# Score matmuls of 64 rows instead of zero-padded ones, values summed key tile by key tile, and a re-planned order, in a kernel of normalized attention and a gated feed-forward layer

## The chip, the cores and the metric

The kernel runs on one core of one Trainium2 chip. The metric is the device time of one execution in microseconds (us). The kernel before was timed three times: 449.11, 449.39 and 452.02 us, median 449.39 us. One more execution was profiled; the profile's times below are of that one.

## The reference: what is computed

There are 8 batches, 12 heads, 448 positions and 64 numbers per head. Attention comes first, then a feed-forward layer over all 3584 tokens:

```
q_n, k_n = rmsnorm(q, g_q), rmsnorm(k, g_k)          # over the 64 numbers of a head
attn = softmax(q_n @ k_n.T / sqrt(64))                # 448 x 448 for each of 96 heads
x = (attn @ v), heads side by side                    # 3584 x 768
h = x @ w_in                                          # 768 -> 2048
out = (h * clip(h + 3, 0, 6) / 6) @ w_out             # 2048 -> 768
```

All inputs and the output are float32 in memory. The matmuls take bfloat16 operands.

## The kernel before

**Pairs.** Two heads are handled together, which fills 2 x 64 = 128 rows; there are 48 pairs, 6 to a batch. The 448 positions of a head are 3 full tiles of 128 rows and a rest of 64. The two rests of a pair share one tile (number 3), so a pair has 7 key tiles: 0 to 2 of the first head, 3 with both rests, 4 to 6 of the second head.

**Stages of a pair.** k, q and v are loaded for two pairs at a time (a group) into rings of three staging buffers `k_st`, `q_st`, `v_st`. `square` (L309) and `stats_sum` (L317) make sums of squares, `stats_rstd` (L323) the factors 1/rms on ACT. `normalize` (L332) multiplies k and q by them. In pairs 0 to 13 (`TD = 14`) `transposes` (L346) turns them on PE into the PSUM tile `t_ps`; `put_q` (L381) and `put_k` (L387) copy them out into `kq`. From pair 14 on a DMA transpose does this instead (`transposes_dma`, L377), into a copy of the same layout that POOL has written, and `scale_q` on ACT multiplies q by the gains.

**The padded k.** The part of `kq` called `kpad` holds 7 blocks of 128 columns. Rows 0 to 63 belong to the first head and rows 64 to 127 to the second. A block of tiles 0 to 2 has the first head's k in the upper rows and zeros below; a block of tiles 4 to 6 the reverse; block 3 holds both rests. q of both heads stands below each other in the same 128 rows. So each score matmul (`score`, L392) contracts over 128 rows, half of them zeros in six cases of seven. `clear_k` (L507) writes the zeros once for each of three ring buffers; `put_k` makes two copies of 64 rows per pair.

**Scores, weights, values.** Each score matmul writes one of two PSUM banks (`sc`), and `expo` (L398) on ACT makes the exponentials `eT` from it, one of a ring of 14. With two banks, score number m waits for exponential m-2. When all seven exponentials of a pair are there, `weigh` (L405) multiplies them with the values and a column of ones: for each of four query tiles seven matmuls, one of 130 columns and six of 65, in two halves of two query tiles. They sum into one PSUM tile `av`. `divide` (L425) on DVE divides by the sums of exponentials, which frees `av`. The result is transposed (`x_out`, by PE until pair 13, by DMA after) into `xT`.

**Feed-forward.** For a finished batch, 16 items of six matmuls (`h_mm`, L460) with `relu` on ACT and `gate` on DVE, and then items of 16 matmuls (`y_mm`, L477), each copied out by ACT or DVE and stored. The weights are loaded in 16 pieces of 768 KB through three buffers `w_st` and cast to bfloat16 by POOL, DVE or ACT; the same three buffers are the source of the DMA transposes from pair 14 on, so pair 14 can be normalized only after the last weight is cast.

**What sets the order.** Nothing runs in the order of the loops. Each piece of work is entered in a list with a key (a due time), the engines that could do it with an assumed time on each, and the pieces it depends on. `Plan.run` (L115) then plays time forward: when an engine is free it takes the ready piece with the smallest key, and each piece goes to the engine where its assumed end (weighted by `PRICE`) is earliest. Ready attention work on PE goes ahead of feed-forward matmuls as long as a credit is not negative; `share` sets how fast feed-forward work refills it. What comes out is a fixed order of instructions on each engine. On the chip each engine runs its list in this order and waits where something is not ready yet; the DMA issues on SP are such a list, too.

## Time and profile before

| view | what it says |
|---|---|
| times | 449.11, 449.39, 452.02 us |
| profiled execution | span 449.5 us from the first to the last instruction |
| PE | busy 424.5 us (94%), 3512 matmuls, first one 9.86 us after the start |
| DVE, ACT, POOL | busy 240.1, 274.8 and 229.7 us (53%, 61%, 51%) |
| score matmuls (L393) | 336, each of 448 columns, 8.2 us of waiting before them |
| feed-forward matmuls (L461, L480) | 768 of 448 columns and 896 of 384 columns |
| value matmuls (L413, L419) | 192 of 130 columns and 1152 of 65 columns |
| exponentials (L399) | 336 on ACT, 175.7 us, 48.6 us of waiting before them |
| copies of k out of `t_ps` (L390) | 28 on DVE, 11.7 us |
| casts of v (L280) | 29 on POOL of 618 ns, 10 on DVE of 1145 ns, 9 on ACT of 627 ns |
| DMA | 73.94 MB, queue q1 69.3% of 16 engines' span |

An instruction's row gives its own duration, from start to end. Matmuls overlap: the next one starts before the last one has ended, so the distance from start to start (the pitch), which the timeline shows, is what a matmul costs when PE is full. "Idle before, releaser" says how long the engine stood still before the instructions of a group, and what ended most of that. The granted clock (PEclk) is the share of full speed at which PE ran.

### The profile page before, as it was taken

The page shows a single profiled execution, that of the slowest core. Times are in us where ns is not written, and L with a number is a line of the kernel's source. Part 1 is how long each engine was busy: PE and PEld are TensorE (multiplying, and loading weights), DVE is VectorE, ACT ScalarE, POOL GpSimd, SP SyncE. Part 2 cuts the span into 40 slices and gives each one's busy share as a digit, 9 for nine tenths or more (in the row PEclk, how much of TensorE's full clock was granted, in tenths as well). Part 3 has the DMA queues.
Part 4 walks back from the last instruction along what each step waited for, and adds up shares of the span by engine and source line. Part 5 has one row for each costly group of instructions (what it writes and reads, how often), then busy time and mean ns, then how long its engine had stood idle before and what let it go on. Part 6 is the DMA issues. An engine that isn't in the chain of part 4 may idle for free.

```text
span 449.5 us, 9164 instructions
## 1 busy us (share of the span) xinstructions
PE 424.5 (94%) x3512; PEld 255.4 (57%) x3512; DVE 240.1 (53%) x428; ACT 274.8 (61%) x581; POOL 229.7 (51%) x251
## 2 busy tenths in 40 slices
PE   0888799899999989999999999999999999999996
PEld 0455366565566555666566565656565655555563
DVE  6899888845474346646444555453433253343321
ACT  2678678853487678878776777777767551132100
POOL 5899999958577766855667467552310000000000
PEclk9999899999999999999999999999999999999999
DMA  6899999981999999999899777955545210110021
GB/s 160 208 295 247 306 294 283 309 296 47 216 229 191 227 231 199 169 232 188 160 184 219 177 176 171 223 140 76 93 106 72 73 26 36 61 45 36 24 83 70
DMA packets 140908, 73.94 MB, mean 164 GB/s; under 512 B 90176, under 2 KB 137280, under 8 KB 140864
## 3 DMA queue, kind: packets, MB, share of 16 engines
q1 hardware_dynamic: 139232, 72.44, 69.3%
q10 hardware_dynamic: 1632, 0.92, 0.8%
q8 instruction: 27, 0.44, 0.4%
q14 instruction: 17, 0.14, 0.1%
HBM read 45.61 MB, written 11.01 MB: 126 GB/s over the span
## 4 chain that ended last, share of the span: by engine, by line
PE 84%; DMA 6%; POOL 2%; DVE 2%; ACT 2%; SPq 1%; issue 1%; POOLq 0%
PE m L461 29%; PE m L480 26%; PE sc L393 11%; PE av L419 7%; PE sc L480 5%; DMA k_st<-in_k_dram 4%; DMA kq<-w_st 3%; PE sc L461 3%; PE av L413 2%; ACT eT L399 2%; POOL qk L333 1%; POOL sq L315 1%; DVE vaug L280 1%; PE t_ps L349 1%; SPq L277 0%
## 5 line engine op out<-in xcount | busy, mean ns | idle before, releaser
L399 ACT ACTIVATE eT<-sc 128x448 bf16<-128x448 f32 x336 | 175.7, 542 | 48.6 <-PE sc L393 44.6
L461 PE MATMUL m<-xT,w_in_sb 128*128 128x448 bf16 x708 | 165.7, 355 | 0.2
L480 PE MATMUL m<-w_out_sb,gT 128*128 128x384 bf16 x768 | 150.0, 326 | 0.0
L393 PE MATMUL sc<-kq 128*128 128x448 bf16 x336 | 115.9, 359 | 8.2 <-ACT eT L399 6.4
L480 PEld LDWEIGHTS <-gT 128*128 128x128 bf16 x896 | 87.2, 98 | 62.3 <-issue 0.5
L461 PEld LDWEIGHTS <-w_in_sb 128*128 128x128 bf16 x768 | 74.1, 98 | 68.8 <-issue 6.0
L472 DVE SCALAR_TENSOR_TENSOR gT<-t_sb,m 128x448 bf16<-128x448 f32 x118 | 73.0, 620 | 72.9 <-ACT t_sb L467 72.4
L467 ACT ACTIVATE t_sb<-m 128x448 f32<-128x448 f32 x118 | 63.7, 541 | 47.3 <-PE m L461 44.3
L318 DVE TENSOR_REDUCE ssq<-sq 128x16 f32<-128x1024 f32 (+1 forms) x56 | 58.3, 1058 | 8.4 <-POOL sq L315 7.1
L359 POOL TENSOR_TENSOR w_st<-k_st,rstd 128x256 bf16<-128x256 f32 x68 | 40.2, 612 | 41.3 <-DMA kq<-w_st 40.6
L280 DVE COPY y_sb<-m 128x384 f32<-128x384 f32 x39 | 21.7, 557 | 61.4 <-PE m L480 61.2
L419 PE MATMUL av<-vaug,eT 128*128 128x65 bf16 x1152 | 54.5, 194 | 0.0
L419 PEld LDWEIGHTS <-eT 128*128 128x128 bf16 x1152 | 50.8, 99 | 4.4 <-issue 0.4
L315 POOL TENSOR_TENSOR sq<-k_st 128x1024 f32<-128x1024 f32 (+1 forms) x24 | 42.4, 1765 | 12.7 <-DMA k_st<-in_k_dram 5.9
L315 POOL TENSOR_TENSOR sq<-q_st 128x1024 f32<-128x1024 f32 (+1 forms) x26 | 44.5, 1710 | 7.1 <-DMA q_st<-in_q_dram 3.5
L393 PEld LDWEIGHTS <-kq 128*128 128x128 bf16 x336 | 31.3, 99 | 27.0 <-issue 4.9
L413 PE MATMUL av<-vaug,eT 128*128 128x130 bf16 x192 | 42.7, 222 | 0.0
L280 POOL CAST vaug<-v_st 128x512 bf16<-128x512 f32 x29 | 17.9, 618 | 45.2 <-PE av L419 44.6
L367 POOL TENSOR_TENSOR w_st<-q_st,rstd 128x512 bf16<-128x512 f32 x34 | 35.4, 1042 | 0.0
L429 DVE TENSOR_TENSOR xn<-av,rden 128x512 bf16<-128x512 f32 x48 | 33.2, 691 | 1.7
L428 DVE RECIPROCAL rden<-av 128x8 f32<-128x8 f32 x48 | 9.8, 205 | 34.1 <-PE av L419 33.7
L375 ACT ACTIVATE kq<-kq,gprime 128x448 bf16<-128x448 bf16 x34 | 22.6, 663 | 5.1 <-DMA kq<-w_st 5.1
(55 smaller groups left out, 222.5 us busy)
## 6 DMA issues: line engine op xcount, KB each, us to landing
out_dram<-y_sb SPq DMA_DIRECT2D x24, 384.0 KB, 2.9
k_st<-in_k_dram SPq DMA_DIRECT2D x23, 384.0 KB, 4.6
v_st<-in_v_dram SPq DMA_DIRECT2D x23, 384.0 KB, 4.6
q_st<-in_q_dram SPq DMA_DIRECT2D x22, 384.0 KB, 4.7
w_st<-in_moe_w_in_dram SPq DMA_DIRECT2D x8, 768.0 KB, 7.6
w_st<-in_moe_w_out_dram SPq DMA_DIRECT2D x8, 768.0 KB, 7.1
out_dram<-y_sb SPq DMA_DIRECT2D x8, 192.0 KB, 2.7
k_st<-in_k_dram SPq DMA_DIRECT2D x46, 32.0 KB, 3.9
```

Source lines behind the costliest of these rows:

```text
L280: (eng.copy if eng is nc.scalar else eng.tensor_copy)(out=out, in_=in_)
L315: eng.tensor_tensor(out=sq, in0=x, in1=x, op=A_MULT)
L318: nc.vector.tensor_reduce(out=ssq_r[(p // GP) % 2][:, a, p % GP:p % GP + n, :].rearrange("p r s -> p (r s)"), in_=sq_r[m][:, 0:n].rearrang ...
L359: eng.tensor_tensor(out=blocks[:, c0:c0 + W4].rearrange("p (t c) -> p t c", t=4)[:, :, h * D:(h + 1) * D], in0=raw(0, p, 1)[:, 0, 4 * h:4 ...
L393: nc.tensor.matmul(out=sc_r[n % 2][:, 0:S], lhsT=kpad[p % NK][:, i * P:(i + 1) * P], rhs=qT_r[p % NK], start=True, stop=True,)
L399: nc.scalar.activation(out=eT_r[n % NE][:, 0:S], in_=sc_r[n % 2][:, 0:S], func=EXP, bias=0.0, scale=1.0,)
L413: nc.tensor.matmul(out=av_ps[:, i, 0:2 * W], lhsT=e[3][:, cols], rhs=va[:, 3].rearrange("p h d -> p (h d)"), start=True, stop=False, skip_ ...
L419: nc.tensor.matmul(out=av_ps[:, i, h * W:(h + 1) * W], lhsT=e[4 * h + t][:, cols], rhs=va[:, t, h], start=False, stop=(t == NT - 1 and h = ...
L461: nc.tensor.matmul(out=m[:, 0:S], lhsT=w_in_sb[:, kt, f * P:(f + 1) * P], rhs=xT[:, kt, b % NX, x_slot(b)], start=(kt == 0), stop=(kt == N ...
L467: nc.scalar.activation(out=t[:], in_=m[:, 0:S], func=RELU, bias=0.5, scale=1.0 / 6.0,)
L472: nc.vector.scalar_tensor_tensor(out=gT[:, f, (b % 2) * S:(b % 2 + 1) * S], in0=t[:], scalar=1.0, in1=m[:, 0:S], op0=A_MIN, op1=A_MULT,)
L480: nc.tensor.matmul(out=m[:, 0:n], lhsT=gT[:, f, c0:c0 + P], rhs=w_out_sb[:, f, c:c + n], start=(f == 0), stop=(f == NFT - 1),)
```

## The change

Pairs 0 to 13 keep k without zero blocks. A score matmul of one head's tile takes the 64 rows of that head alone; tile 3, with both rests, still takes 128. For this the second head's rest is loaded to another place of `k_st`, three more small memsets clear what stays empty there, and `raw` picks the slots. `put_k` becomes one copy of 128 rows by 512 columns, on DVE or ACT, and `clear_k` is gone. Pairs from 14 on keep their layout and their 128-row score matmuls.

The key tiles are taken in the order 3, 0, 4, 1, 5, 2, 6. `weigh` is called once for each key tile, right when its exponential is there, and adds that tile's share to all four query tiles. An exponential's buffer is free for reuse after its own `weigh` instead of the whole pair's.

The planner is given other assumed times, most of them shorter, and a fixed extra time (`LAG`) between the end of an instruction on POOL, ACT or DVE and the start of what depends on it. Score matmuls get the smallest key, -1. The extra 100 or so lines of the diff that only change such numbers are cut:

```diff
+    LAG = {"POOL": 45, "ACT": 105, "DVE": 85}
...
-        op.end = now + ns + op.lag
+        op.end = now + ns + (op.lag or self.LAG.get(engine, 0))
...
-        for rows, x, t, rest in zip((lo, hi), (0, 0), (NT, 4), halves_of(src)):
+        for rows, x, t, rest in zip((lo, hi), (0, 1 if p < TD else 0), (NT, NT if p < TD else 4), halves_of(src)):
...
-    def put_k(p, part):
-        kp = kpad[p % NK]
-        rows, c0 = ((lo, 0), (hi, NT * P))[part]
-        nc.vector.tensor_copy(out=kp[rows, c0:c0 + 4 * P], in_=t_ps[rows, 0, :])
+    def put_k(eng, p):
+        copy(eng, out=kpad[p % NK][:, 0:W4], in_=t_ps[:, 0, :])

     def score(p, i, n):
+        if p >= TD or i == NT:
+            rows, c0 = slice(0, P), i * P
+        else:
+            rows, c0 = ((lo, i * P), (hi, (i - 4) * P))[i > NT]
         nc.tensor.matmul(
-            out=sc_r[n % 2][:, 0:S], lhsT=kpad[p % NK][:, i * P:(i + 1) * P],
-            rhs=qT_r[p % NK], start=True, stop=True,
+            out=sc_r[n % 2][:, 0:S], lhsT=kpad[p % NK][rows, c0:c0 + P],
+            rhs=qT_r[p % NK][rows, :], start=True, stop=True,
         )
...
-    def weigh(p, half):
...
+    def weigh(p, n):
+        va, i = vaug[p % NV], ORDER[n]
+        e = eT_r[(7 * p + n) % NE]
+        first, last = n == 0, n == len(ORDER) - 1
+        for j in range(4):
+            c0 = j * P if (p // HP) % 2 == 0 else (j * P - P if j else S - P)
+            if i == NT:
+                out, rhs = av_ps[:, j, 0:2 * W], va[:, NT].rearrange("p h d -> p (h d)")
+            else:
+                h, t = divmod(i, 4)
+                out, rhs = av_ps[:, j, h * W:(h + 1) * W], va[:, t, h]
             nc.tensor.matmul(
-                out=av_ps[:, i, 0:2 * W], lhsT=e[3][:, cols], rhs=va[:, 3].rearrange("p h d -> p (h d)"),
-                start=True, stop=False, skip_group_check=True,
+                out=out, lhsT=e[:, c0:c0 + P], rhs=rhs,
+                start=first and j % 2 == 0, stop=last, skip_group_check=True,
             )
...
-    def clear_k(eng, i):
-        eng.memset(kpad[i][D:P, 0:3 * P], 0.0)
-        eng.memset(kpad[i][0:D, 4 * P:7 * P], 0.0)
...
-    ORDER = (0, 1, 2, 3, 4, 5, 6)
+    ORDER = (3, 0, 4, 1, 5, 2, 6)
...
-        vc.append(add((p, 5), [("DVE", 700, lambda p=p: cast_v(V, p)),
-                               ("POOL", 640, lambda p=p: cast_v(G, p)),
-                               ("ACT", 640, lambda p=p: cast_v(A_, p))],
-                      [lv[p], at(wgh, 2 * (p - NV) + 1), at(clo, p)]))
+        vc.append(add((p, 5), [("DVE", 1350, lambda p=p: cast_v(V, p)),
+                               ("POOL", 575, lambda p=p: cast_v(G, p)),
+                               ("ACT", 530, lambda p=p: cast_v(A_, p))],
+                      [lv[p], at(wgh, 7 * (p - NV) + 6), at(clo, p)]))
...
-            scs.append(add((p, 2), [("PE", 189, lambda p=p, i=i, m=m: score(p, i, m))],
-                           [pq[p], pk[2 * p], pk[2 * p + 1] if i >= 3 else None, at(exs, m - 2)], 165))
-            exs.append(add((p, 1), [("ACT", 550, lambda m=m: expo(m))],
-                           [scs[m], at(wgh, 2 * ((m - NE) // 7) + 1) if m >= NE else None]))
-        for half in range(2):
-            wgh.append(add((p + 1, 1), [("PE", 510, lambda p=p, half=half: weigh(p, half))],
-                           exs[7 * p:7 * p + 7] + [vc[p], at(div, p - 1), pad], 165))
+            scs.append(add((-1, p), [("PE", 189, lambda p=p, i=i, m=m: score(p, i, m))],
+                           [pq[p], pk[p], at(exs, m - 2)], 165))
+            exs.append(add((p, 1), [("ACT", 440, lambda m=m: expo(m))],
+                           [scs[m], at(wgh, m - NE)]))
+        for n in range(7):
+            wgh.append(add((p + 1, 1), [("PE", 240 if ORDER[n] == NT else 132, lambda p=p, n=n: weigh(p, n))],
+                           [exs[7 * p + n], vc[p], at(div, p - 1), pad, wgh[-1] if n else None], 165))
```

The other assumed times that the change alters, before and after in ns: `relu` 550 and 440, `gate` 600 and 540, output copies on ACT 480 and 375 and on DVE 560 and 475, weight casts on DVE 1500 and 2500, `normalize` on POOL 1150 and 1000 and on DVE 1250 and 1400, `put_q` on DVE 450 and 370 and on ACT 640 and 450.

85 lines of the change are left out of this document (37 added, 48 removed).

## The prediction

> **What bounds the kernel now.** I read the page first: busy shares, the 40 slices, the groups.
>
> ```profile
> span 449.5 us, 9164 instructions
> ...
> PE   0888799899999989999999999999999999999996
> ...
> DVE  6899888845474346646444555453433253343321
> ...
> POOL 5899999958577766855667467552310000000000
> PEclk9999899999999999999999999999999999999999
> DMA  6899999981999999999899777955545210110021
> ```
>
> PE is full from the sixth slice on; before that POOL, DVE and DMA are. So I need the price of a matmul when PE is full, which is its pitch, not its duration. The PE timeline gives it:
>
> ```profile
> 199.77 0.35 PE L393 MATMUL sc<-kq 128*128 128x448 bf16 x1
> 199.96 0.54 PE L461 MATMUL m<-xT,w_in_sb 128*128 128x448 bf16 x2
> 200.34 0.35 PE L393 MATMUL sc<-kq 128*128 128x448 bf16 x1
> ...
> 202.04 0.22 PE L413 MATMUL av<-vaug,eT 128*128 128x130 bf16 x1
> ...
> 203.04 0.35 PE L393 MATMUL sc<-kq 128*128 128x448 bf16 x1
> ```
>
> A score matmul lasts 0.35, but the next starts 0.19 later: 0.16 is hidden under its successor. The 28 value matmuls of a pair take 203.04 - 202.04 = 1.00. The chain of waits has 42 matmuls of L461 in 7.94 (0.189 each) and 32 of L480 in 5.20 (0.1625). All of PE: 768 x 0.189 + 896 x 0.1625 + 336 x 0.189 + 48 x 1.00 + 168 transposes x 0.056 = **412**. The last matmul ends at 445.8; with 0.56 for the last copy and the last store the span is 449.5. So PE loses 449.5 - 412 - 3.9 = 33.6, and the place of the loss follows from the instruction order: the pitches of all matmuls ahead of a pair's first score, against the time at which it started. Lost until pair 6: 43.2 - 19.1 = 24.0; pair 7: 53.2 - 24.6 = 28.6; pair 8: 29.2; pair 13: 31.6; pair 14: 118.9 - 87.2 = 31.6; pair 21: 33.6; nothing more after. The two lines of PE and two of DVE that carry the jump at pair 7:
>
> ```profile
> 47.08 0.40 PE L446 MATMUL m<-identity,xn 128*128 128x128 bf16 x4 [1.74 <-DVE xn L429]
> ...
> 49.21 3.15 PE L461 MATMUL m<-xT,w_in_sb 128*128 128x448 bf16 x8
> ```
>
> ```profile
> 42.65 2.85 DVE L280 CAST vaug<-v_st 128x512 bf16<-128x512 f32 x2
> ...
> 46.33 0.69 DVE L429 TENSOR_TENSOR xn<-av,rden 128x512 bf16<-128x512 f32 x1
> ```
>
> Two casts of v on DVE delay the quotient, PE waits, and then runs eight matmuls at 0.39 instead of 0.19 (clock 0.89 in 45 to 60 us).
>
> The profiled execution's span (449.5) and the median of the runs (449.39) are the same within 0.1, so the sum below stands for both. A difference of under 1% (4.5 us) I count as no change that can be told.
>
> **The change, part by part.** Counts are from the built order of both programs.
>
> *Number of matmuls*: 3512 in both, with the same columns. 412 stays, if no pitch changes.
>
> *DVE and POOL.* DVE loses its 10 casts of v (11.4), and 28 copies of 0.417 become 13 of the same length per row (-6.3); four `put_q` and one copy go to ACT (+2.6 by the 0.66 and 0.42 rows). POOL gets 13 casts of 0.62 (+8), loses three squares of 1.9 and one of 1.0 (-6.7) and two memsets (-0.8), so it is even. ACT takes those squares and sheds three casts and four output copies (-3.8); it is busy 12 of 15 us in 30 to 45, so this hides there, and if it did not, it would be some 3. The new memsets of k (three of 0.165) stand on DVE where four of 0.22 went, ahead of the first sum at 6.0, which waits for ACT's square until 5.84. The jam at pair 7 goes. What is late next is DMA: it is at 0.97 to 1.12 of its 16 engines from 30 to 75 us, the order of loads on SP is the same up to there, and k and q of pairs 8 and 9 come at about 39 and 41 (POOL starts their square at 39.29). From 41: square of q 1.9, sum 1.2, 1/rms 0.5, two normalizations with a weight cast between 3.5, transposes 0.6, two copies on ACT behind three `relu` 2.7: pair 8 starts at about 51.5. Of matmuls 27.5 lie ahead of it now (30.7 before), so 24 to 25 is lost, **24.5** against 29.2. From there to pair 14 all inputs come earlier than PE asks (pair 14 has 92.2 of matmuls ahead, so it is asked for at 117; its transposed k was there at 114.4 before): 0 more.
>
> *Matmuls of 64 rows.* 84 scores of pairs 0 to 13 have a tile of another shape than what runs around them. PE changes between the shapes 146 times, 70 of these from pair 8 on, where PE is full. No row of before shows two shapes on PE. Below: nothing, as between different lines of the same shape (pitch 0.19), or a gain where an upper and a lower half run side by side; but with two score banks they are mostly apart, only 11 times does one half follow the other directly, so at most 11 x 0.19 = 2. Above: the overlap of 0.16 is lost and the weight load (0.098) cannot run ahead, 0.26 a change. I take **0.16**, the row nearest to a matmul that has to be through before one of another shape may start: 70 x 0.16 = 11.2. The 76 changes before pair 8 fall where PE waits anyway (2.3 of matmuls in 5.1 per pair); they cost 1.5, through scores that come later to ACT. The Trainium skill, TensorEngine Tiling (Array Packing), section Key Properties, says that changing the tiling mode, not just the tile, drains the TensorE. It gives no time for this; by it the change costs something, and without it nothing; nothing in the trace of before can agree or disagree.
>
> *Values by key tile.* Same 28 matmuls, in seven fours. A four follows any matmul at the usual pitch (0.19 after L461, 0.032 after L419). Each four now waits for one exponential, with score and feed-forward matmuls queued behind it on PE; before, 28 waited for seven. From 110 us on the planner leaves 0.5 between ACT's end and what needs it on PE, before that 0.06 plus the new `LAG` of 0.105. The assumed 440 for an exponential is what the trace shows from start to start when ACT is not kept waiting (0.49 for some in the start). Cost: **0.6** over the run, bounds 0 and 3.
>
> *The new pace from pair 14 to 27.* 168.7 - 92.2 = 76.5 of matmuls for 13 pairs, 5.9 a pair; before 6.8. SP must issue per pair: transposes 1.41 + 1.23, half of three k issues 0.88, of two q 0.58, of three v 0.88, stores 0.35, gaps 0.4: 5.7. When SP was full before, PE waited, behind ACT, which stood still for the transposed k:
>
> ```profile
> 160.89 0.67 ACT L375 ACTIVATE kq<-kq,gprime 128x448 bf16<-128x448 bf16 x1 [1.04 <-DMA kq<-w_st]
> ```
>
> A pace of 6.3 is my estimate, between the 5.7 of the issues and the 6.9 a pair that these 13 pairs took before: 13 x 6.3 - 76.5 = 5.4 lost, and **4.5** when PE comes later anyway. Bounds 0 and 15 (7.08 a pair, what pairs 17 to 21 took in landings). Before it was 2.0. After pair 27 the pace is 7.3, which SP has kept.
>
> *End*: last copy and store 3.9, as before.
>
> **Sum**: 412.0 + 24.5 + 1.5 + 11.2 + 0.6 + 4.5 + 3.9 = **458**.
>
> **The rivals.**
> - *The changes of shape are free* (0.43 is for my case, 0.27 for this). Then 412 + 24.5 + 0.6 + 5.4 + 3.9 = 446.5, not slower. For it: the trace hides the weight loads and the ends of all matmuls. It decides from 0.05 a change down: 70 x 0.05 = 3.5 brings 450. Its own range is 442.5 to 450.
> - *The weight load is exposed too*, 0.26 a change: 70 x 0.26 = 18.2, and 3 in the start: 412 + 24.5 + 3 + 18.2 + 0.6 + 4 + 3.9 = 466. Chance 0.12.
> - *SP and DMA become the bound.* Changes of shape free, but 13 pairs at 7.08: 15.5 lost, 456.5. Against: SP's issues in 165 to 210 us were 12.4 of 15 at 7.1 a pair, so there was room. Chance 0.10.
> - Something else (the planned order starves an engine, or it fits better than I think): 0.08.
>
> **How the numbers follow.** My case holds 453 to 463 as the bubble goes from 0.1 to 0.2. The range 443 to 466 leaves out the lowest of the free case, the upper half of the exposed load, and most of the rest: 0.18. Faster by over 1% (under 444.9): 0.10 of the free case and 0.05 of the rest, 0.15. Within 1%: 0.17 of the free case, 0.06 of mine, 0.03 of SP, 0.26. Slower: 0.59.
>
> **What would show it.** Right: score matmuls of pairs 8 to 13 whose successor starts 0.3 to 0.4 later, not 0.19, and fours of value matmuls that start late behind them; pair 8's first score at 51 to 53; more waiting of ACT for `kq` in 120 to 200 us; v casts gone from DVE. Wrong: a pitch of 0.19 around 64-row scores, or pair 8 later than 56, which would say that the start is not held by DMA as I read it.

## The result, and the profile after

The changed kernel takes **471.89 us** (median of four runs, 470.42 to 473.47) beside 449.52 us for the kernel before on the same chip: 1.047 times as long, with a 95% interval of 1.043 to 1.051. The forecast was 458, in a range of 443 to 466. The sign was right, the size was not.

First the page of the changed kernel, the same parts as for the kernel before: the span, then the busy share of each engine in 40 slices of 11.7 us.

```profile
span 469.3 us, 9136 instructions
...
PE   0899999999999989879899999999999999999996
...
DVE  6444756765445435663555463563434254343411
...
POOL 3957796775757776777785567542401000000000
PEclk9999999999999999999999999999999999999999
DMA  6798898947089989999978988868354321000031
```

DVE has lost its nines in the first 60 us, as forecast. PE is at nine tenths from the third slice on (before from the sixth), and yet the kernel is 20 us longer: PE is busy with something that takes longer. There is a dent in slices 15 to 20 (164 to 235 us) that was not there before.

The measure of the forecast, the time lost at the first score of a pair (its start, less the pitches of all matmuls ahead of it), says where the 20 us are:

```
first score of     before: start  lost     after: start  lost    changes of shape so far
pair 2                     23.2   18.0             24.3   19.3    16
pair 5                     38.9   22.7             46.5   32.0    50
pair 8                     59.9   29.2             64.6   37.0    76
pair 14                   118.8   31.6            136.4   44.2   146
pair 28                   215.9   33.6            229.3   54.3   146
last matmul               445.8   33.7            465.5   53.5   146
```

Up to pair 8 the changed kernel loses 7.8 more than before, from there to pair 14 4.7 more, from 14 to 28 8.1 more, and behind that 0.9 less. The three parts have three causes.

**From pair 8 to pair 14** PE is full. This is its timeline in that stretch (start, duration, line, operation, tile and shape, number of instructions):

```profile
78.69 0.35 PE L466 MATMUL m<-xT,w_in_sb 128*128 128x448 bf16 x1
78.98 0.36 PE L400 MATMUL sc<-kq 64*128 64x448 bf16 x1
79.27 0.74 PE L466 MATMUL m<-xT,w_in_sb 128*128 128x448 bf16 x3
...
81.41 0.61 PE L354 MATMUL t_ps<-identity,qk 128*128 128x128 bf16 x8
81.95 0.36 PE L400 MATMUL sc<-kq 64*128 64x448 bf16 x1
82.24 0.30 PE L425 MATMUL av<-vaug,eT 128*128 128x65 bf16 x4
```

From the feed-forward matmul to the 64-row score and from there to the next are 0.29 each, in place of 0.19 between matmuls of one shape. Over the whole stretch the median pitches are 0.285 and 0.292. So **a change of shape costs 0.10**, and the 70 changes from pair 8 on make 7.15 of loss.

**In the start** everything on PE takes double. The same eight transposes, 54 us earlier in the same kernel:

```profile
26.94 1.04 PE L354 MATMUL t_ps<-identity,qk 128*128 128x128 bf16 x8
27.91 0.55 PE L400 MATMUL sc<-kq 64*128 64x448 bf16 x1
28.39 0.40 PE L425 MATMUL av<-vaug,eT 128*128 128x65 bf16 x4
```

0.97 for the eight where it was 0.54 at 81.41. The first clock record in the trace is a grant of full speed at 47.07 us; in the kernel before it is at 21.60. The row PEclk above shows nines from its first slice, though: it has nothing to show ahead of the first record. The half clock is seen in the pitches.

**From pair 14 to 28** PE waits for ACT, and ACT for a transposed k. One line of the timeline of PE, one of that of ACT:

```profile
225.18 0.35 PE L400 MATMUL sc<-kq 128*128 128x448 bf16 x1 [2.31 <-ACT eT L406]
```

```profile
223.59 0.67 ACT L380 ACTIVATE kq<-kq,gprime 128x448 bf16<-128x448 bf16 x1 [3.17 <-DMA kq<-w_st]
```

These are the waits that the forecast had read in the kernel before (there 1.04); here the longest is 3.17.

### The profile page after: what moved, and what is told of

Same layout as the page of the kernel before. It is cut to its first block, busy times and chain, and to the rows that moved or that the text cites. A ratio compares the mean times of both kernels' runs of the same rounds, so it can differ in the third digit from the quotient of the medians.

```text
span 469.3 us, 9136 instructions
## 1 busy us (share of the span) xinstructions
PE 442.2 (94%) x3512; PEld 254.5 (54%) x3512; DVE 222.8 (47%) x403; ACT 275.4 (59%) x583; POOL 228.6 (49%) x257
## 2 busy tenths in 40 slices
DMA packets 140908, 73.94 MB, mean 158 GB/s; under 512 B 90176, under 2 KB 137280, under 8 KB 140864
## 4 chain that ended last, share of the span: by engine, by line
PE 80%; DMA 7%; POOL 3%; ACT 2%; DVE 2%; issue 2%; SPq 1%; POOLq 0%; ACTq 0%; DVEq 0%
PE m L485 24%; PE m L466 23%; PE sc L400 13%; PE av L425 9%; PE sc L485 4%; DMA kq<-w_st 4%; DMA k_st<-in_k_dram 3%; PE sc L466 3%; POOL sq L320 2%; PE t_ps L354 2%; ACT eT L406 1%; DMA gk_t<-in_g_k_dram 1%; POOL w_st L364 1%; SPq L271 1%; DVE ssq L323 1%
## 5 line engine op out<-in xcount | busy, mean ns | idle before, releaser
L466 PE MATMUL m<-xT,w_in_sb 128*128 128x448 bf16 x696 | 173.6, 354 | 2.3 <-DVE gT L477 2.1
L485 PE MATMUL m<-w_out_sb,gT 128*128 128x384 bf16 x768 | 158.9, 326 | 0.0
L400 PE MATMUL sc<-kq 128*128 128x448 bf16 (+1 forms) x336 | 123.6, 374 | 9.0 <-ACT eT L406 5.7
L425 PEld LDWEIGHTS <-eT 128*128 128x128 bf16 x1344 | 85.2, 100 | 59.5 <-issue 12.7
L485 PEld LDWEIGHTS <-gT 128*128 128x128 bf16 x896 | 81.9, 98 | 47.3 <-issue 0.9
L425 PE MATMUL av<-vaug,eT 128*128 128x65 bf16 (+1 forms) x1344 | 101.8, 202 | 1.8 <-DVE xn L434 1.8
L466 PEld LDWEIGHTS <-w_in_sb 128*128 128x128 bf16 x768 | 67.3, 98 | 52.5 <-issue 10.3
L400 PEld LDWEIGHTS <-kq 128*128 128x128 bf16 (+1 forms) x336 | 32.0, 97 | 33.1 <-issue 12.9
L282 POOL CAST vaug<-v_st 128x512 bf16<-128x512 f32 x42 | 25.9, 618 | 45.3 <-PE av L425 45.3
L380 ACT ACTIVATE kq<-kq,gprime 128x448 bf16<-128x448 bf16 x34 | 22.6, 665 | 13.3 <-DMA kq<-w_st 12.9
L433 DVE RECIPROCAL rden<-av 128x8 f32<-128x8 f32 x48 | 9.8, 205 | 28.4 <-PE av L425 28.3
L485 PE MATMUL sc<-w_out_sb,gT 128*128 128x384 bf16 x128 | 21.8, 326 | 0.0
```

Source lines behind the costliest of these rows:

```text
L282: (eng.copy if eng is nc.scalar else eng.tensor_copy)(out=out, in_=in_)
L400: nc.tensor.matmul(out=sc_r[n % 2][:, 0:S], lhsT=kpad[p % NK][rows, c0:c0 + P], rhs=qT_r[p % NK][rows, :], start=True, stop=True,)
L425: nc.tensor.matmul(out=out, lhsT=e[:, c0:c0 + P], rhs=rhs, start=first and j % 2 == 0, stop=last, skip_group_check=True,)
L466: nc.tensor.matmul(out=m[:, 0:S], lhsT=w_in_sb[:, kt, f * P:(f + 1) * P], rhs=xT[:, kt, b % NX, x_slot(b)], start=(kt == 0), stop=(kt == N ...
L485: nc.tensor.matmul(out=m[:, 0:n], lhsT=gT[:, f, c0:c0 + P], rhs=w_out_sb[:, f, c:c + n], start=(f == 0), stop=(f == NFT - 1),)
```

## The experiments

The last three columns are the time lost at the first scores of pairs 8, 14 and 28, read as above from the one profiled execution of each kernel; the times are medians of four or ten runs, where the table does not say one. The kernel before took 450.4 to 450.9 us (medians) beside them. Summary first, in the order in which they are told:

```
run               us       against before (95%)    clock  lost at pair 8 / 14 / 28
changed kernel    471.89   1.047 (1.043 to 1.051)  47.07  37.0  44.2  54.3
a1_full_rows      455.79   1.012 (1.007 to 1.017)  17.22  26.4  27.9  39.3
b1_half_rows      459.10   1.022 (1.014 to 1.030)  22.18  30.9  40.1  40.9
a3_padded         456.14   1.011 (1.002 to 1.019)  17.70  27.0  27.8  38.8
a5_warm           464.69   1.030 (1.023 to 1.037)  see text
a6_grouped        471.60   1.045 (1.038 to 1.052)  38.87  33.6  40.8  53.4
a2_pace           467.63   1.037 (1.032 to 1.043)  39.06  33.8  40.9  46.9
a7_light          471.68   one run                 47.06  37.2  44.4  54.8
a8_light_all      466.76   one run                 41.49  34.7  41.8  49.7
a9_no_tails       461.50   one run                 47.37  37.1  44.2  44.5
a4_padded_pace    453.68   1.007 (1.004 to 1.010)  19.02  27.4  28.2  35.3
d1_land           450.90   0.999 (0.996 to 1.002)  20.62  26.7  27.5  32.0
d2_vload_act      454.65   1.010 (1.006 to 1.013)  19.46  27.3  31.0  40.0
d3_land_pace      452.48   1.004 (1.002 to 1.007)  20.29  27.7  28.5  35.8
b2_values         452.67   1.006 (1.003 to 1.009)  18.96  28.2  30.0  35.3
b3_vcast          451.05   1.004 (1.001 to 1.007)  17.46  28.6  32.2  32.6
b4_vcast_warm     455.97   1.012 (1.008 to 1.016)   7.08  27.5  31.0  33.3
d4_before_land    450.99   0.999 (0.996 to 1.002)  16.89  24.9  29.9  32.0
```

"Clock" is the time of the first grant of full speed.

### Is it the 64 rows, or the new order?

**The changed kernel with full rows.** The order is the changed kernel's; the keys of the two heads are mixed in the scores.

```diff
-            rows, c0 = ((lo, i * P), (hi, (i - 4) * P))[i > NT]
+            rows, c0 = slice(0, P), (i * P, (i - 4) * P)[i > NT]
```

> The changed kernel, order and waits untouched, but the scores of pairs 0 to 13 contract all 128 rows of the unpadded k (the keys of both heads are mixed in these scores, so only the time counts). Theory (shape): the 64-row matmuls themselves cost the time, in two ways, a bubble of 0.10 at each change of shape and a tensor clock that stays at half until 47 us. Then the clock is granted from about 21 us as before the change, the first score of pair 8 starts near 54 with some 26 to 29 lost, the pitch of a score is 0.19 between any neighbours, and the kernel takes 454 to 458 (471.9 less 7.2 for the changes from pair 8 on and less 7 to 10 for the start). Rival (order): the clock stays low because the new plan, with the values key tile by key tile, feeds the tensor engine otherwise; then the clock still comes at about 47 and only the bubbles go, 463 to 465.

Measured: 455.79 us. The clock is granted at 17.22, pair 8 has 26.4 lost (37.0 with half rows), and from there to pair 14 1.5 (7.15). PE's timeline there:

```profile
23.27 0.61 PE L354 MATMUL t_ps<-identity,qk 128*128 128x128 bf16 x8
23.72 0.35 PE L400 MATMUL sc<-kq 128*128 128x448 bf16 x1
23.91 0.28 PE L425 MATMUL av<-vaug,eT 128*128 128x65 bf16 x4
```

The eight transposes take 0.45 at 23 us, not 0.97. What the rows do in this order is worth 16 us. The loss behind pair 14 stays (11.4, of which a spell at half clock from 160.58 to 163.99 is up to 1.7): that one has nothing to do with the rows.

**The kernel before with half rows.** The other direction: order, padded k and loads of before, but only the 64 rows that are not zero are read.

```diff
+        rows = slice(0, P) if p >= TD or i == NT else lo if i < NT else hi
-            out=sc_r[n % 2][:, 0:S], lhsT=kpad[p % NK][:, i * P:(i + 1) * P],
-            rhs=qT_r[p % NK], start=True, stop=True,
+            out=sc_r[n % 2][:, 0:S], lhsT=kpad[p % NK][rows, i * P:(i + 1) * P],
+            rhs=qT_r[p % NK][rows, :], start=True, stop=True,
```

> The kernel before, order untouched, but the scores of pairs 0 to 13 read only the 64 rows of the padded k that are not zero (same result). Theory (shape): the clock comes much later than 21.6 us, and every change of shape costs 0.10; 14 pairs with 6 half scores each that mostly stand apart give about 146 changes, some 70 of them where the tensor engine is full: 7 us, and 7 to 10 in the start, 463 to 467. Rival (order): the clock still comes at about 21.6 us and only the bubbles are added, 456 to 458. If neither shape nor bubble counts outside the new order, 449 to 451.

Measured: 459.10 us. The order changes shape 98 times, 53 of them from pair 8 on, and they cost what they cost in the changed kernel:

```profile
71.88 0.54 PE L462 MATMUL m<-xT,w_in_sb 128*128 128x448 bf16 x2
72.36 0.36 PE L394 MATMUL sc<-kq 64*128 64x448 bf16 x1
72.65 0.40 PE L447 MATMUL t_ps<-identity,xn 128*128 128x128 bf16 x4
```

(0.29 from the score to the transposes.) Between pair 8 and 14 the loss is 9.2, 6.8 more than before: 53 x 0.10 = 5.3, and one spell at half clock from 93.86 to 97.28, which is 1.7. But the clock comes at 22.18, and the start loses only 1.7 more than before. So my theory (463 to 467, a late clock) fell in part: in the order of before, half rows do not hold the clock back, and the rival (456 to 458) comes nearer. What else it takes is told below, as far as a fit can.

**Streams by themselves.** A kernel that only runs matmuls of 448 columns (and, in its last two parts, four of 65 columns to each of them); it computes nothing of the reference. `lo` and `hi` are the lower and upper 64 rows, `full` all 128.

```diff
+        for n in range(60):
+            mm(lo, n, S, rhs)
...
+        for n in range(60):
+            mm((lo, full)[n % 2], n, S, rhs)
...
+        for n in range(60):
+            mm(full, n, S, rhs)
+        for n in range(40):
+            mm((lo, full)[n % 2], n, S, rhs)
+        for n in range(40):
+            mm(lo, n, S, rhs)
+        for n in range(40):
+            mm((lo, hi)[n % 2], n, S, rhs)
...
```

> A measurement by itself, nothing of the reference is computed: streams of 448-column matmuls, with 26 copies on ACT (some 10 us of a still tensor engine) between them. In order: 60 of 64 rows alone; 60 of 64 and 128 rows in turn; 60 of 128 rows, then 40 of 64 and 128 rows in turn, 40 of 64 rows, 40 of lower and upper 64 rows in turn; then 30 times one of 64 rows and four of 128 rows by 65 columns; then the same with one of 128 rows. Theory (shape lowers the clock): a stream of 128 rows is granted the full clock after a few us, a stream of 64 rows or of both in turn stays at half for far longer or for good; and the pitch in turn is 0.19 plus 0.10 at full clock, lower and upper halves in turn about 0.1 each. Rival (only still time counts): all streams get the full clock after the same few us, and the late clock in the changed kernel comes from its gaps.

Measured, as its theory expected (but the stretches of still PE were not there: ACT had made its copies ahead, and the streams follow each other within 0.4 us). Its table by windows: stretch, then length, busy time and number of instructions of PE, of its weight loads, of DVE, ACT and POOL, then the granted clock (1.00 even ahead of its first record, as said above), the share of the DMA engines and GB/s.

```profile
6.00:26.00 20.00, 20.00 (x55) 7.95 (x54) 0.00 (x0) 19.04 (x32) 0.00 (x0) 1.00 1.00 392
28.00:55.00 27.00, 27.00 (x57) 5.79 (x56) 0.00 (x0) 25.72 (x43) 0.00 (x0) 1.00 0.23 89
58.00:67.00 9.00, 9.00 (x49) 4.70 (x48) 0.00 (x0) 8.55 (x15) 0.00 (x0) 1.00 0.00 0
69.00:79.00 10.00, 10.00 (x36) 3.21 (x35) 0.00 (x0) 2.64 (x5) 0.00 (x0) 1.00 0.01 2
87.20:91.00 3.80, 3.80 (x42) 1.90 (x38) 0.00 (x0) 0.00 (x0) 0.00 (x0) 1.00 0.00 0
```

From start to start: 64 rows alone 0.373, in turn with 128 rows 0.487, both until 56 us; then 128 rows 0.189, in turn 0.294, 64 rows alone 0.189, lower and upper half in turn 0.10 (0.171 and 0.019: a pair of halves runs side by side). A stream of 64 rows without a gap ran for 22 us, and one of both in turn for 29 us, at half clock. The grant came at 57.27, 1.2 us after the first matmul of the stream of 128 rows. Once granted, the clock stayed for the 7.2 us of 64 rows alone. At half clock a change of shape costs 0.11, at full clock 0.10; a stream of one shape, 64 rows included, costs nothing extra.

The Trainium skill, TensorE: Matmul & The Clock Gate, section Part 1: The HAM clock gate (the "warmup" mystery), says that the clock is released after a window of about 3.4 us in which PE was busy. The half spells in these traces do last 3.41 us or a multiple of it, so the window agrees; but "busy" is not enough, as 22 us of busy 64-row matmuls show. The Trainium skill, TensorEngine Tiling (Array Packing), section Key Properties, says that a change of tiling mode drains the TensorE, which the forecast had cited without a time for it. The trace agrees: a change costs 0.10, and a stream that stays in one mode pays none.

**What the clock counts.** From every profile here I cut the time into windows of 3.41 us that end where the clock changes, and took the share of each in which PE streams columns (0.42 ns a column, 0.83 at half clock, from the pitches of 0.189 and 0.373 for 448 columns), with 128-row matmuls at 1 and 64-row ones at weight w:

```
windows at half clock, all profiles    w = 0        w = 1/2      w = 1
clock granted at the end (35)          0.62 and up  0.73 and up  0.75 and up
not granted (155)                      up to 0.77   up to 0.77   up to 1.00
```

With w = 1/2 the two sets part at 0.73 to 0.75, but for one or two windows at that edge that were not followed by a grant; with 1 they overlap widely. And with w = 1/2 a granted clock is taken away after windows of 0.36 or less (15), never after 0.38 or more (2349 windows); with w = 0 it would have been kept through windows of 0.00, in the stream of 64 rows alone. Weights from some 0.4 to 0.7 do nearly as well, so the half is a round figure. This is a fit to these traces, no more; no run changed the share by itself. By it both kernels can be understood: in the changed one the windows between 20 and 43 us reach 0.56 to 0.70, since a third of the time goes to half rows that count half, and the first with 0.83 ends at 47.07; in the kernel before with half rows the window up to 22.18 holds most of a run of 28 value matmuls, eight transposes and a score of tile 3, and reaches 0.83.

**Warmed up.** The order of the changed kernel, with matmuls of the identity before and between.

```diff
+        if p < 2:
+            warm(3)
...
+        for _ in range(n):
+            nc.tensor.matmul(out=m_r[0][:, 0:P], lhsT=identity[:], rhs=identity[:], start=True, stop=True)
...
+        warm(100)
         plan.run()
```

> The changed kernel, order untouched, with 100 matmuls of the identity with itself (128 rows, 128 columns) on the tensor engine from 1.3 us on, while it has nothing to do, and three more behind each score of pairs 0 and 1. Theory: the clock is granted before 10 us and kept, the matmuls of the start run at 0.19 in place of 0.37, and what stays of the loss at pair 8 are the bubbles: 29 to 34 in place of 37.0, in all 464 to 469. Rival: the 64-row scores lose the clock again as soon as the additional matmuls end, and it comes back at 40 to 47; 470 to 473.

Measured: 464.69 us, 7.2 less than the changed kernel. The row of the granted clock by slices:

```profile
PEclk9589999999999999999999999999999999999999
```

Granted at 5.43, taken away at 12.26, when PE had mostly waited, and granted again at 25.91. Between the two theories, then: it was lost, but through waiting, and it came back 21 us earlier than without. Pair 8 starts at 59.9 in place of 64.6. The added matmuls take time, too: the first score of pair 2 comes at 28.3 in place of 24.3. So what the clock is worth has to be read behind that, from the first score of pair 2 to that of pair 5. The changed kernel runs this stretch at half clock, the other two at full:

```
from pair 2 to 5    us    pitches at full clock  changes of shape  PE idle
changed kernel      22.2  9.4                    34                0.3
warmed up           13.8  9.4                    34                0.6
full rows           13.3  9.4                    0                 1.6
```

At half clock PE is what this stretch waits for: 2 x 9.4 of pitches and 34 x 0.11 for the changes make 22.5, so each change counts. At full clock the same half rows and changes take 0.5 more than full rows do, and PE waits less in their place. Two rows of the warmed kernel in this stretch, the eight transposes between half rows, now 0.56 from start to start with the change behind them:

```profile
29.93 0.62 PE L354 MATMUL t_ps<-identity,qk 128*128 128x128 bf16 x8
30.49 0.36 PE L400 MATMUL sc<-kq 64*128 64x448 bf16 x1
```

From pair 5 to 8 the three differ little (18.1, 17.8, 18.8). So of the 10.6 that the start of the changed kernel loses beyond full rows, 8.9 lie between pairs 2 and 5, and 8.4 of these go when the clock is there and the half rows stay. One thing is not separated: the warmed kernel comes to pair 2 later than the one with full rows (28.3 and 21.9), so its loads are further ahead of PE.

**Values grouped.**

```diff
-                           [exs[7 * p + n], vc[p], at(div, p - 1), pad, wgh[-1] if n else None], 165))
+                           [*(exs[7 * p:7 * p + 7] if p < TD else exs[7 * p + n:7 * p + n + 1]), vc[p], at(div, p - 1), pad, wgh[-1] if n else None], 165))
```

> The changed kernel planned anew with one difference: in pairs 0 to 13 the fours of value matmuls wait for all seven exponentials of their pair, as the 28 did before the change, so that 64-row scores stand less between them. Theory (it takes both: half rows, and full-row matmuls cut into short pieces between them): changes of shape fall from 146 to about 100 and the clock comes at 20 to 30 as in the kernel before with half rows; pair 8 with 30 to 33 lost, 463 to 467. Rival (half rows in this plan suffice): the clock still comes at 39 or later, 468 to 472.

Measured: 471.60 us. The plan came out with the same order on every engine as the changed kernel's. Score matmuls go ahead of everything, so the fours of pairs 0 to 13 never ran before the last exponential of their pair, and what stands between the half rows are fours of the pair before. So that its time lies in the rival's range says nothing for the rival: it is the changed kernel again, and the question is not decided by it. What it does tell is the scatter of the clock: in six profiles of this start the grant came between 38.87 and 47.37, and pair 8 started between 61.2 and 64.8. Eight us of clock are worth 3.4 there.

### What of the rest of the change?

**The new plan with padded k.** Loads, memsets, two copies and 128-row scores of before; everything else of the change stays.

```diff
-        if p >= TD or i == NT:
-            rows, c0 = slice(0, P), i * P
-        else:
-            rows, c0 = ((lo, i * P), (hi, (i - 4) * P))[i > NT]
+        rows, c0 = slice(0, P), i * P
...
-            pk.append(add((p - 1, 1), [("DVE", 370, lambda p=p: put_k(V, p)), ("ACT", 500, lambda p=p: put_k(A_, p))],
-                          [tr[p], at(scs, 7 * (p - NK) + 6)]))
+            for part in range(2):
+                pk.append(add((p - 1, 1 + part), [("DVE", 415, lambda p=p, part=part: put_k(p, part))],
+                              [tr[p], at(scs, 7 * (p - NK) + 6), at(clk, p)]))
```

> The changed kernel with the padded k of before for pairs 0 to 13 (loads, memsets, two copies of k on DVE, 128-row scores, planned anew), but the values key tile by key tile, the key order 3, 0, 4, 1, 5, 2, 6 and all planner numbers of the change. Theory: without 64-row scores nothing is left of the bubbles and of the late clock, so the first score of pair 8 has 26 to 28 lost, pair 14 has 27 to 30, and the 10 of pairs 14 to 27 stay; 454 to 457. So the rest of the change is worth 5 to 8 us more than before's order up to pair 14 (31.6 lost there) and gives it back behind it. Rival: the new order needs the single copy of k and stalls on DVE with the two; pair 8 at 29 or more, 458 or more.

Measured: 456.14 us, as expected point by point: 27.0, 27.8, and 11.0 lost between pair 14 and 28. Unpadded k saved a copy per pair on DVE, and that is worth at most 0.6 here: with two copies the loss at pair 8 is 27.0, with full rows over one copy 26.4. The new plan gains 3.8 against before up to pair 14 and loses 9.0 behind it.

**Parts of the change on the kernel before.** Values by key tile alone, the numbers of the v casts alone, and these with a warm-up:

```diff
-        for half in range(2):
-            wgh.append(add((p + 1, 1), [("PE", 510, lambda p=p, half=half: weigh(p, half))],
+        for n in range(7):
+            wgh.append(add((p + 1, 1), [("PE", 240 if ORDER[n] == NT else 132, lambda p=p, n=n: weigh(p, n))],
```

> The kernel before with one part of the change: values key tile by key tile and the key order 3, 0, 4, 1, 5, 2, 6; padded k, 128-row scores and all planner numbers of before. Theory: summed by key tile the values are worth something in the start, since the exponentials of a pair are consumed one by one: loss at pair 8 of 27 to 29 in place of 29.2, at pair 14 of 28 to 31 in place of 31.6, and with the pace of before 1 to 3 lost behind: 446 to 450. Rival: the gain in the start of the kernel with padded k and the new plan comes from the planner's numbers, and values by key tile alone are worth nothing: 449 to 453.

```diff
-        vc.append(add((p, 5), [("DVE", 700, lambda p=p: cast_v(V, p)),
-                               ("POOL", 640, lambda p=p: cast_v(G, p)),
-                               ("ACT", 640, lambda p=p: cast_v(A_, p))],
+        vc.append(add((p, 5), [("DVE", 1350, lambda p=p: cast_v(V, p)),
+                               ("POOL", 575, lambda p=p: cast_v(G, p)),
+                               ("ACT", 530, lambda p=p: cast_v(A_, p))],
```

> The kernel before with one part of the change: the planner's numbers for the casts of v (DVE 1350, POOL 575, ACT 530 in place of 700, 640, 640), which take these casts off DVE. Theory: the 4.6 that are lost between pair 6 and 7 behind two casts of v on DVE go, and part of it comes back as waiting for POOL; 445 to 449. Rival: the pairs come no sooner, since the loads set the start: 448 to 451.

> As the kernel before with the new numbers for the casts of v, with 100 identity matmuls on the tensor engine from 1.3 us on and three behind each score of pairs 0 and 1. Theory: the clock is granted before 10 us, lost once while the tensor engine waits, and back by 18 to 22, no later than without; the start gains 0 to 2 us, 444 to 449. Rival: the additional matmuls stand ahead of scores that PE was late for: 0 to 2 slower than without them.

Measured: 452.67, 451.05 and 455.97 us; none is faster than before, and the first two came out as their rivals had it. Values by key tile gain 1.6 up to pair 14 and lose 3.3 more behind it. Without the v casts on DVE pair 7 comes at 50.1 in place of 53.2, but mostly because its plan puts 2.5 less of matmuls ahead of it; 28.0 are lost there in place of 28.6, and at pair 14 0.6 more than before. The last one is slower than both its expectations, and its profiled execution (459.05 us, the longest of four) shows a reason that neither had. First the timeline of its DVE, then of its POOL:

```profile
46.07 6.27 DVE L333 TENSOR_TENSOR qk<-k_st,rstd 128x512 bf16<-128x512 f32 x1
52.27 0.20 DVE L434 RECIPROCAL rden<-av 128x8 f32<-128x8 f32 x1
```

```profile
45.08 1.90 POOL L315 TENSOR_TENSOR sq<-k_st 128x1024 f32<-128x1024 f32 x1
...
49.33 0.62 POOL L280 CAST vaug<-v_st 128x512 bf16<-128x512 f32 x1
49.90 1.90 POOL L315 TENSOR_TENSOR sq<-q_st 128x1024 f32<-128x1024 f32 x1
55.84 1.04 POOL L333 TENSOR_TENSOR qk<-k_st,rstd 128x512 bf16<-128x512 f32 x1 [4.04 <-ACT rstd L328]
```

One normalization on DVE took 6.27 us where this operation takes 0.7 to 1.9 in every other case of these profiles. POOL ran beside it without a pause until 51.80, and the normalization ended half a microsecond after that; PE stood still for 5.0 behind the quotient that was queued on DVE. The Trainium skill, Trainium Architecture — The Big Picture, section What this means for kernel authors, says that VectorE and GpSimd share a pair of ports to SBUF under an exclusive lock. This one row agrees with that, but nothing here shows that the lock was the cause, or how often it strikes. So this run says nothing on warming up: its clock was granted at 7.08, taken at 13.90, back at 20.73 and lost again in that wait.

### Why do pairs 14 to 27 lose 10 us?

**A slower pace** for these pairs, on the changed kernel:

```diff
-    plan = Plan(share=(2.0, 1.0, 0.65, 3.0, 0.45))
+    plan = Plan(share=(2.0, 1.0, 0.5, 3.0, 0.45))
```

> The changed kernel with the planner's share for pairs 14 to 27 at 0.5 in place of 0.65: feed-forward matmuls are dealt out more slowly against those of the pairs reversed, that is, fewer pairs per unit of feed-forward work, so that a pair takes longer. Theory (pace): the 10.1 us that are lost from pair 14 to pair 28 come from pairs that are asked for faster than transposes and loads on the SP queue deliver them; at the slower pace the loss there falls to 2 to 4 and the kernel takes 464 to 467. Rival (engines): the loss comes from the order on ACT and DVE in this stretch, and stays at 8 or more at the slower pace too; 470 to 474. The start is the same in both.

Measured: 467.63 us; 6.0 are lost there, not 10.1, so four tenths of it go. Its clock also came at 39.06, worth 3.2 of the difference. Neither theory had this.

**Fewer bytes.** Large loads of q, k and v cut to half of the partitions, same number of issues, in one run for pairs 14 to 27, in a second for all from 14 on. The edit of the second:

```diff
+        part = lo if p >= TD else slice(0, P)
-        eng.dma_start(out=dst[:, :, 0:NT, :].rearrange("p h t d -> p h (t d)"), in_=blocks(src))
+        eng.dma_start(out=dst[part, :, 0:NT, :].rearrange("p h t d -> p h (t d)"), in_=blocks(src)[part])
```

> The changed kernel, order and number of issues untouched, but the loads of q, k and v of pairs 14 to 27 bring only half of the partitions of their large part (what stays in the buffers is old data, so only the time counts). Theory (bytes): the DMA engines are what sets the pace of these pairs; with half of the load bytes the loss from pair 14 to pair 28 falls from 10.1 to 0 to 4, and the transposes of pair 17 to 27 come every 5.9 to 6.2 us in place of 6.6. Rival (issues and order on SP, and what waits behind the sums on DVE): as many issues in the same order, so a loss of 7 to 10 stays and the transposes come every 6.4 or more. Up to pair 14 nothing changes but for the window in which the clock comes.

> The changed kernel, order and number of issues untouched, with the large parts of the loads of q, k and v of all pairs from 14 on cut to half of the partitions (only the time counts; the first such run cut them for pairs 14 to 27 only, and from 180 us on full loads of later pairs stood in the same queue). If bytes set the pace, the loss from pair 14 to pair 28 falls to 0 to 5. If it is SP, which hands out its transfers one behind the other, it stays at 7 to 11.

**Fewer issues.** The small loads of the last 64 positions, five of the eight issues of two pairs and few of their bytes, are left out from pair 20 on.

```diff
+        if p < 20:
+            eng.dma_start(out=dst[lo, :, NT, :], in_=src[:, FULL:S, :].rearrange("h p d -> p h d"))
-        eng.dma_start(out=dst[lo, :, NT, :], in_=src[:, FULL:S, :].rearrange("h p d -> p h d"))
```

> The changed kernel, order otherwise untouched, but from pair 20 on the five small loads of the last rows of each two pairs of q, k and v are left out (of eight issues for each two pairs three are left and nearly all bytes; only the time counts). If SP's time to hand out transfers sets the pace, each pair needs 2.5 issues of 0.65, that is 1.6 us, less, and the loss from pair 20 to pair 28, 10.4 in the changed kernel, falls to 0 to 4. If it is bytes, it stays at 8 to 11.

Measured, the windows of the changed kernel, of the second one with fewer bytes and of the one with fewer issues (stretch, length, busy time of PE, of its weight loads, of DVE, ACT and POOL, clock, share of the DMA engines, GB/s):

```profile
136.00:170.00 34.00, 34.00 (x333) 22.12 (x331) 14.55 (x22) 26.72 (x58) 26.66 (x28) 1.00 0.94 218
170.00:230.00 60.00, 51.25 (x441) 29.25 (x437) 31.32 (x49) 43.78 (x99) 42.12 (x44) 1.00 0.94 201
```

```profile
136.00:170.00 34.00, 34.00 (x339) 22.09 (x337) 15.00 (x22) 26.83 (x58) 26.84 (x27) 1.00 0.82 169
170.00:230.00 60.00, 53.06 (x449) 30.43 (x446) 32.24 (x52) 46.55 (x104) 44.30 (x47) 1.00 0.83 163
```

```profile
136.00:170.00 34.00, 34.00 (x333) 22.09 (x332) 14.36 (x22) 26.65 (x58) 27.02 (x29) 1.00 1.08 250
170.00:230.00 60.00, 59.32 (x516) 35.13 (x513) 37.12 (x56) 52.16 (x115) 47.97 (x50) 1.00 0.90 188
```

With fewer bytes PE still stands still for 6.9 of 60 us, though the DMA engines fell to 0.83; 7.9 are lost between pair 14 and 28 (10.4 in the first of the two runs, 1.7 of it a spell at half clock). With fewer issues PE is full, the loss is 0.3, and the kernel 10 us shorter, while the DMA engines move as much as in the changed kernel (250 and 188 GB/s in the two stretches, where it was 218 and 201). Both cuts leave about as many packets (127852 and 129035 of 140908 in the whole kernel), so it is not their number either. In this order it is the number of issues, then, though each cut is one run. All of these stand in one list on **SP**, which hands out one transfer after another. Its timeline in the changed kernel:

```profile
187.68 1.77 SPq L383 DMA_TRANSPOSE kq<-w_st  x1
189.54 1.28 SPq L455 DMA_TRANSPOSE xT<-xn  x1
190.92 0.54 SPq L268 DMA_DIRECT2D k_st<-in_k_dram  x1
191.51 1.28 SPq L271 DMA_DIRECT2D k_st<-in_k_dram  x2
192.89 1.43 SPq L383 DMA_TRANSPOSE kq<-w_st  x1
194.41 0.71 SPq L259 DMA_DIRECT2D q_st<-in_q_dram  x1
195.18 0.63 SPq L260 DMA_DIRECT2D q_st<-in_q_dram  x1
195.90 0.55 SPq L277 DMA_DIRECT2D v_st<-in_v_dram  x1
```

One follows the other within 0.1 us. From the transposes of pair 17 (145.36) to those of pair 27 (211.21) are 65.85 us, 6.6 a pair, and SP has 0.43 us in all in which it is between issues for longer than that. With fewer issues it has some 12. Not all of the 6.6 is handing out: the two transposes of a pair take 1.61 and 1.57 in the mean and 1.31 and 1.22 at the least, because SP waits inside some of them (its waits before `kq` transposes lead the list, for scores that still read the buffer). That is 11 x 0.30 + 10 x 0.35 = 6.8 us, so by this estimate SP's own time is 5.9 a pair and 0.7 is waiting. Leaving the small loads out also lets a square start after one landing in place of two or three; no run separates that from SP's time.

**Away from SP, and later in the plan.** Five kernels. Three have padded k and the new plan: one with a slower pace (a4); one with the loads of v issued by ACT (d2); one with 1.5 us more assumed for each transfer after 110 us, so that what needs a load is planned later, and a share of 0.50 (d1). The fourth is the third with a share of 0.40 (d3). The fifth is the kernel before with values by key tile, the new numbers of the v casts and the same 1.5 us (d4).

```diff
-    plan = Plan(share=(2.0, 1.0, 0.65, 3.0, 0.45))
+    plan = Plan(share=(2.0, 1.0, 0.4, 3.0, 0.45))
```

> As the kernel with padded k and the new plan, and the planner's share for pairs 14 to 27 at 0.40 in place of 0.65. Theory (transfers set the pace of these pairs at some 93 to 97 us for 14 pairs, whatever is asked; what PE is asked for sooner is lost): asked for at 97 or more the loss there falls from 10 to 0 to 3, and the kernel takes 445 to 449, faster than both. Rival (order on ACT and DVE): a loss of 6 or more stays, as at a share of 0.5, and it takes 451 or more.

```diff
+                ve, vq = (nc.scalar, "ACT") if p >= TD else (nc.sync, "SP")
-                lv_g[p0] = plan.dma((p0 + (VL if g == 0 else 0), 2), 3, n * kb, lambda p0=p0, n=n: load_v(nc.sync, p0, n), oldv)
+                lv_g[p0] = plan.dma((p0 + (VL if g == 0 else 0), 2), 3, n * kb, lambda p0=p0, n=n, ve=ve: load_v(ve, p0, n), oldv,
+                                    queue=vq)
```

> The kernel with padded k and the new plan, share 0.65, with the loads of v from pair 14 on issued by ACT in place of SP (planned so). Theory (SP's time to hand out transfers): a pair needs 1 us less of SP, 5.3 in place of 6.3, and the loss from pair 14 to 28 falls from 11 to 2 to 5, less what three issues for two pairs cost on ACT: 447 to 451. Rival (bytes, or ACT, which is busy for 8 of 10 us there and now issues too): 8 or more are lost, 453 to 458.

```diff
-            op.end = max(op.end, self.free["pipe"] + op.lag)
+            op.end = max(op.end, self.free["pipe"] + op.lag + (1500 if now > self.STEADY else 0))
```

> The kernel with padded k and the new plan, share 0.50 for pairs 14 to 27, and 1.5 us more assumed by the planner for every transfer that is issued after 110 us, so that what needs a load stands later in the orders of DVE, POOL and ACT. Theory (the sums on DVE, which wait for a late load, hold back quotients that are queued behind them): the loss from pair 14 to 28 falls from 7 to 11 to 0 to 4; 446 to 450. Rival (SP's own time): 5 or more are still lost; 451 to 456.

> The kernel with padded k, the new plan and 1.5 us more assumed for each late transfer, with the share for pairs 14 to 27 at 0.40 in place of 0.50. Theory (SP needs some 6.5 us for a pair; asked for at 7.3 nothing is late, if the order of DVE leaves room for late loads): 27.5 lost at pair 14 and 0 to 2 more behind it, 445 to 449, faster than both kernels by 0 to 1%. Rival (the lost time behind pair 19 comes from the order, whatever the pace): 3 to 5 more are lost, 449 to 453.

> The kernel before with values key tile by key tile, the new planner numbers for the casts of v, and 1.5 us more assumed for each late transfer; padded k and the other numbers of before. Theory: 28 to 30 lost at pair 14 and 1 to 3 behind it, 446 to 450. Rival: as the two parts alone, 450 to 453.

Measured, in the order a4, d2, d1, d3, d4: 453.68, 454.65, 450.90, 452.48 and 450.99 us. The slower pace (a4) still loses 7.1 behind pair 14, most of it around pair 20, as its rival expected. ACT as a second issuer (d2) loses 9.0, as its rival expected, 5.5 of it between pairs 19 and 20 in waits for ACT and at the half clock that followed; SP stood between issues for some 12 us from pair 17 to 27, as with fewer issues, so a free SP was not enough there. The longer assumed landing loses 4.5 at a share of 0.50 (d1, between its two expectations), and 7.3 at 0.40 (d3): slower pace and later plan do not add up. The theory for d3 failed; its rival had the time (449 to 453), but 3 to 5 for the loss. For d4 the profiled execution lost what the theory said (29.9 at pair 14, 2.1 behind it), but the median is the rival's. So SP's list, its waits included, holds the changed kernel at 6.6 a pair, where leaving out issues ended the loss; why other orders lose 3 to 6 around pair 20, at any pace and with SP free, I can only point at. In one of them (full rows) DVE waited 5.1 us for a square and then for the sum that was queued ahead of a quotient, and PE 2.5 for that quotient. It was not tried by itself and stays open.

No version beats the kernel before by what can be measured: the best two, 450.90 and 450.99, have intervals of 0.996 to 1.002 around it.

## Why the prediction was wrong, step by step

- **412 of pitches**: held. The loss computed with them is the same wherever PE is full, and drifts by 0.8 behind pair 28 only because the value matmuls of 65 columns follow each other at 0.030, not 0.0325.
- **24.5 lost till pair 8**: right but for 2, if the 64-row matmuls are taken out: 26.4 with full rows, pair 8 at 54.0 (forecast 51.5). The reading that loads set this start held. The sign named for the opposite, "pair 8 later than 56", came true (64.6), for another reason.
- **1.5 for changes of shape in the start: this is the step that failed.** In its place 10.6 were lost beyond full rows. The forecast let these 76 changes fall "where PE waits anyway", from the matmuls per pair at full clock. It did not ask whether the clock would still come when the matmuls that had earned it shrank to half their rows, though its own trace showed a half clock once, at 45 to 60 us. The clock came at 47.07 in place of 21.60. Up to then PE ran at half speed and was what the start waits for: 22.2 us from pair 2 to 5, where the warmed kernel, with the same changes, took 13.8 and full rows 13.3. So some 8.4 of the 10.6 are the clock, with the changes made dear by it. Changes alone cost about what the forecast said: in the kernel before with half rows, whose clock came at 22.18, 45 of them ahead of pair 8 cost 1.7.
- **70 x 0.16 = 11.2 from pair 8 on**: right mechanism, size off: 70 x 0.102 = 7.15. The successor of a score started 0.29 later, just under the 0.3 to 0.4 that were named as a sign. The row it was taken from, the 0.16 that a matmul hides under its successor, was not the right one. The rival with the weight load exposed (0.26 a change, 466) came nearest to the time with a wrong mechanism; "free" fell.
- **0.6 for the value fours**: nothing of it is seen apart. In pairs 0 to 13, and from 27 on, all fours still ran behind the last exponential of their pair; in pairs 14 to 26 the first ones ran 1.5 to 4 us ahead of it.
- **4.5 for the pace of pairs 14 to 27**: mechanism right, size off: 10.1. SP's time was put at 5.7 a pair and the pace at 6.3; the pace came out at 6.6. The transposes were put at 1.41 + 1.23 and take 1.61 + 1.57, with the 0.7 of waits inside them that the estimate left out, and eight issues, the store and the gaps add the rest (3.4 where 3.1 was put). SP's own time, 5.9, is close to the 5.7. The rival that gave it 7.08 a pair had it too high.
- **3.9 for the end**: 3.8.

Put together with what was measured: 412 + 37.0 + 7.15 + 10.1 - 0.8 + 3.8 = 469.3, the span. Of the 19.8 by which that is longer than before, 7.8 came by pair 8, 4.7 on the way to pair 14 and 8.1 behind it. The errors of the forecast are +11.0, -4.0 and +5.6, less 1.5 for the fours, the drift and the end together.

## What to carry to other kernels

A matmul on half of the rows streams as many columns in the same time; it saves nothing on PE unless an upper and a lower half run next to each other, and where PE is full each change between it and full-row work costs 0.10 us, so count the changes in the built order, not the matmuls. Before a matmul is made smaller in a start that waits for data, ask what had released the clock, and read the clock from pitches: the row of the granted clock shows nothing ahead of its first record. For a queue that hands out transfers in order, add up the issues per unit of work, with the waits inside them, against the pace that is asked for; halving the bytes left 7.9 and 10.4 of the loss of 10.1 here, in one run each, and dropping five small issues of eight left 0.3.

## What was not expected of the hardware

- 22 us of 64-row matmuls without a gap did not bring the full clock, nor did 29 us of 64 and 128 rows in turn; 1.2 us of 128 rows behind them did. By the fit above, a matmul of 64 rows counts about half, a window of 3.41 us had to reach some 0.73 to 0.75, so weighted, and a granted clock went after windows under 0.37.
- A change between 64-row and 128-row matmuls costs 0.10 us at full and 0.11 at half clock, for matmuls of 448 as of 65 columns; two halves in turn run side by side, 0.19 for both.
- One normalization on DVE lasted 6.27 us beside a POOL that did not pause, in one execution.
